# Moving the transposes of q, k and the attention output from TensorE to the DMA crossbar, from the third token block on

## The chip, the cores and the metric

The kernel runs on one core of a Trainium2 chip. The metric is the device time in microseconds (us). The engines are named as in the profile: PE is TensorE (matmuls), PEld its weight loads, DVE is VectorE, ACT is ScalarE, POOL is GpSimd and SP is SyncE, which in this kernel does nothing but issue DMA transfers, one after the other in a fixed order. "L234" is line 234 of the kernel that the profile belongs to.

Each kernel was run several times. All comparisons below are of fast runs; one run counted as slow (of `g6_early_ring_store`, 365.85 us) and is left out of its ratio.

## The reference, cut to what matters

```python
# q, k, v: (8, 8, 576, 64) float32; w_in: (512, 2048); w_out: (2048, 512)
scores = scale * q @ k.T                       # per batch and head
mask   = (rel >= 0) & (rel < 64)               # sliding window of 64, causal
attn   = softmax(where(mask, scores, -1e9))
x      = (attn @ v) laid out as (4608 tokens, 512)
out    = square(maximum(x @ w_in, 0)) @ w_out
```

## The kernel before

The 4608 tokens are 36 tiles of 128 tokens, and 4 tiles make a block of 512 tokens; there are 9 blocks, numbered 0 to 8. In phase g the kernel runs the second FFN matmul (`ops`) of block g-1 and the first (`hps`) of block g on TensorE, weaves the attention of block g+1 in between, and loads q, k and v of block g+2. The order of the instructions on each engine is fixed when the kernel is built.

The score matmuls read q and k with the head dimension over the partitions (`sc<-qT,kT 64*128` in the timelines), and the first FFN matmul reads the attention output x with its 512 columns over the partitions, in four parts (`hps<-xT,w_in_sb 128*128`), so all three are transposed. Before the change TensorE does it, with an identity as second operand, into PSUM. VectorE and ScalarE copy the results back to SBUF.

```python
def load(i):                                    # tile i: three loads on SP, then casts on GpSimd
    for (src, nm) in ((k, "k"), (q, "q"), (v, "v")):
        st = stage.tile([P, H, D], FP32, name=f"{nm}_st", tag="st")
        nc.sync.dma_start(out=st[:], in_=src[b0, :, ...].rearrange("h p d -> p h d"))
    ...                                         # (a tile on the seam of two batches takes two loads each)
    nc.gpsimd.tensor_copy(out=k16s[i][:], in_=...)          # float16 copies k16, q16, v_ev, v_od
    ...

def transposes(i):
    ps = ps_att.tile([P, 2, HP, P], FP16, name="qkT_ps", tag="ps_a")
    for s, src in enumerate((k16s, q16s)):
        for hp in range(HP):                    # HP = 4
            nc.tensor.transpose(out=ps[:, s, hp, :], in_=src[i][:, hp * P:(hp + 1) * P],
                                identity=ident[:])
    kT = attw.tile([P, HP, 192], FP16, name="kT", tag="kT")
    if i > 0:                                   # the last 64 columns of the tile before
        nc.vector.tensor_copy(out=kT[:, :, 0:64], in_=kTs[i - 1][:, :, P:192])
    ...
    nc.vector.tensor_copy(out=kT[:, :, 64:192], in_=ps[:, 0])
    qT = attw.tile([P, HP, P], FP16, name="qT", tag="qT")
    nc.scalar.activation(out=qT[:], in_=ps[:, 1], func=AF.Copy, scale=1.0)

def to_xT(i):
    xt = ps_att.tile([P, DMC, P], FP16, name="xt_ps", tag="ps_a")
    for c in range(DMC):                        # DMC = 4
        nc.tensor.transpose(out=xt[:, c, :], in_=xs[i][:, 2 * c:2 * c + 2, :], identity=ident[:])
    nc.vector.tensor_copy(out=xT_of(i // 4)[:, :, (i % 4) * P:(i % 4 + 1) * P], in_=xt[:])

def ffn_out(g):
    ...
    nc.sync.dma_start(out=out[...], in_=osb[:])  # the store is on SP too

for g in range(NTB + 1):                        # NTB = 9
    streams = []
    if g > 0:        streams.append((ffn_out(g - 1), 0.0, 1.0))
    if g < NTB:      streams.append((ffn_up(g), 0.0, 1.0))
    ...
    if g + 1 < NTB:  streams.append((attention(g + 1), 0.0, 0.95))
    if g + 2 < NTB:  streams.append((loads(g + 2), 0.6 if g == 0 else 0.0, 1.0))
    for s in weave(*streams):
        s()
```

The softmax here doesn't subtract the row's maximum and nothing guards it: scores larger than these inputs give would overflow.

## Time and profile before

| before the change | value | read from |
|---|---|---|
| time, median of 4 runs | 351.89 us (351.73 to 352.61) | the runs |
| TensorE busy | 322.0 us, 92% of the span | page, part 1 |
| one token block | 34.0 us | timeline of PE |
| time of one transposed tile (3 packs of 4) on PE | 0.67 us | timeline of PE |
| DMA engines, mean busy share | 57% | page, part 3 |
| TensorE idle between 84 and 310 us | 0.05 us | windows |

The first lines are from the page of the kernel before: busy time by engine; then the span in 40 slices of 8.8 us, each digit a busy share in tenths (PEclk is the granted TensorE clock); then the DMA queue with packets, MB and its share of the 16 engines' time; then the chain of waits that ended last, by engine.

```profile
PE 322.0 (92%) x2736; PEld 161.3 (46%) x2736; DVE 202.0 (57%) x485; ACT 180.9 (51%) x321; POOL 118.3 (34%) x196
...
PE   1458786999999999999999999999999999999995
...
PEclk9999898799999999999999999999999999999999
DMA  8927995799999456838999779400000000100021
...
q1 hardware_dynamic: 122304, 46.15, 56.9%
...
PE 82%; DMA 5%; DVE 4%; POOL 4%; ACT 2%; issue 1%; SPq 1%; ACTq 0%; POOLq 0%
```

TensorE is at 90% or more in every slice from the ninth to the last but one, at full clock, and it is 82% of the chain that ended last: it is the limit. The DMA engines fall idle after slice 26: by about 227 us all of q, k and v has been loaded, so the loads run ahead of their use.

The next lines are the timeline of PE in the kernel before (start, duration, engine, line, operation, destination from sources, shapes, count).

```profile
183.38 0.39 PE L166 MATMUL qkT_ps<-ident,k_2666 128*128 128x128 f16 x4
183.61 0.39 PE L166 MATMUL qkT_ps<-ident,q_2668 128*128 128x128 f16 x4
183.83 1.03 PE L261 MATMUL ops<-w_out_sb,h_2165 128*128 128x512 f16 x4
```

Matmuls overlap, so a pack of four transposes costs the distance from its start to the next start, 0.22 to 0.23 us, and not its 0.39 us. A tile has three packs.

### The profile page before, as it was taken

What the parts mean: (1) busy time and instruction counts of PE and PEld (TensorE: products, weight loads), DVE (VectorE), ACT (ScalarE), POOL (GpSimd) and SP (SyncE); (2) the same over time, 40 slices, a digit from 0 to 9 for tenths busy, and PEclk for the clock granted to TensorE, in tenths of its full rate; (3) what the DMA queues carried; (4) which work ended last, traced back from release to release, by engine and by line L of the source; (5) the groups of instructions that cost most, each with busy time, mean ns of one, the idle gap of its engine ahead of it and who ended that gap; (6) DMA issues with size and microseconds to landing.
All of it is one profiled execution on the core that took longest, in us unless ns stands there. A gap on an engine that the chain in (4) does not pass through costs nothing.

```text
span 351.8 us, 7118 instructions
## 1 busy us (share of the span) xinstructions
PE 322.0 (92%) x2736; PEld 161.3 (46%) x2736; DVE 202.0 (57%) x485; ACT 180.9 (51%) x321; POOL 118.3 (34%) x196
## 2 busy tenths in 40 slices
PE   1458786999999999999999999999999999999995
PEld 0343234544555445544554454445445544444442
DVE  1464358545967665667576756665576566643300
ACT  2346666695646444654555355536653664344421
POOL 5960175008867334426576634440000000000000
PEclk9999898799999999999999999999999999999999
DMA  8927995799999456838999779400000000100021
GB/s 176 219 106 227 219 216 158 217 267 208 219 243 229 91 122 156 181 95 190 199 203 184 155 156 202 108 32 32 30 32 30 33 32 30 61 31 30 32 81 69
DMA packets 122338, 46.60 MB, mean 132 GB/s; under 512 B 113600, under 2 KB 113600, under 8 KB 122304
## 3 DMA queue, kind: packets, MB, share of 16 engines
q1 hardware_dynamic: 122304, 46.15, 56.9%
q8 instruction: 21, 0.34, 0.4%
q14 instruction: 13, 0.11, 0.1%
HBM read 36.70 MB, written 9.44 MB: 131 GB/s over the span
## 4 chain that ended last, share of the span: by engine, by line
PE 82%; DMA 5%; DVE 4%; POOL 4%; ACT 2%; issue 1%; SPq 1%; ACTq 0%; POOLq 0%
PE ops L261 36%; PE hps L243 33%; PE av L204 4%; PE qkT_ps L166 4%; DMA k_st<-in_k_dram 3%; PE xt_ps L217 2%; DMA ws<-in_moe_w_in_dram 2%; ACT hrelu L247 1%; DVE h_580 L248 1%; DVE x_sb L209 1%; SPq L144 1%; DVE kT L173 1%; ACT qT L175 1%; DVE h_1086 L248 0%; DVE rden L208 0%
## 5 line engine op out<-in xcount | busy, mean ns | idle before, releaser
L243 PE MATMUL hps<-xT,w_in_sb 128*128 128x512 f16 x576 | 152.0, 385 | 5.6 <-DVE h_580 L248 4.7
L247 ACT ACTIVATE hrelu<-hps 128x512 f32<-128x512 f32 x144 | 85.8, 597 | 110.2 <-PE hps L243 109.4
L243 PEld LDWEIGHTS <-w_in_sb 128*128 128x128 f16 x576 | 56.5, 99 | 73.9 <-issue 10.3
L266 ACT ACTIVATE osb<-ops 128x512 f32<-128x512 f32 x36 | 21.5, 599 | 20.5 <-PE ops L261 20.5
L175 ACT ACTIVATE qT<-qkT_ps 128x512 f16<-128x512 f16 x36 | 21.5, 596 | 19.7 <-DVE kT L173 19.7
L173 DVE COPY kT<-qkT_ps 128x512 f16<-128x512 f16 x36 | 15.2, 422 | 26.1 <-PE qkT_ps L166 26.1
L209 DVE TENSOR_TENSOR x_sb<-av,rden 128x256 f16<-128x256 f32 x72 | 27.7, 415 | 0.3
L219 DVE COPY xT<-xt_ps 128x512 f16<-128x512 f16 x36 | 15.1, 420 | 15.3 <-PE xt_ps L217 15.3
L208 DVE RECIPROCAL rden<-av 128x4 f32<-128x4 f32 x72 | 11.9, 180 | 16.7 <-PE av L204 16.5
L248 DVE SCALAR_TENSOR_TENSOR h_4808<-hps,hrelu 128x512 f16<-128x512 f32 x16 | 11.1, 692 | 16.6 <-ACT hrelu L247 16.6
L261 PE MATMUL ops<-w_out_sb,h_580 128*128 128x512 f16 x64 | 19.4, 399 | 0.0
L248 DVE SCALAR_TENSOR_TENSOR h_580<-hps,hrelu 128x512 f16<-128x512 f32 x16 | 11.0, 690 | 13.1 <-ACT hrelu L247 13.1
L184 PEld LDWEIGHTS <-kT 64*128 64x128 f16 x576 | 11.7, 99 | 14.9 <-issue 12.4
L261 PE MATMUL ops<-w_out_sb,h_1086 128*128 128x512 f16 x64 | 16.7, 380 | 0.0
L261 PE MATMUL ops<-w_out_sb,h_2165 128*128 128x512 f16 x64 | 16.5, 380 | 0.0
L261 PE MATMUL ops<-w_out_sb,h_1627 128*128 128x512 f16 x64 | 16.5, 380 | 0.0
L261 PE MATMUL ops<-w_out_sb,h_3244 128*128 128x512 f16 x64 | 16.5, 380 | 0.0
L261 PE MATMUL ops<-w_out_sb,h_2706 128*128 128x512 f16 x64 | 16.5, 380 | 0.0
L261 PE MATMUL ops<-w_out_sb,h_3785 128*128 128x512 f16 x64 | 16.5, 380 | 0.0
L261 PE MATMUL ops<-w_out_sb,h_4322 128*128 128x512 f16 x64 | 16.4, 379 | 0.0
L248 DVE SCALAR_TENSOR_TENSOR h_1086<-hps,hrelu 128x512 f16<-128x512 f32 x16 | 11.0, 688 | 9.1 <-ACT hrelu L247 9.1
L217 PE MATMUL xt_ps<-ident,x_sb 128*128 128x128 f16 x144 | 15.8, 236 | 0.3 <-DVE x_sb L209 0.3
(743 smaller groups left out, 549.2 us busy)
## 6 DMA issues: line engine op xcount, KB each, us to landing
out_dram<-osb SPq DMA_DIRECT2D x36, 256.0 KB, 2.1
k_st<-in_k_dram SPq DMA_DIRECT2D x32, 256.0 KB, 4.6
q_st<-in_q_dram SPq DMA_DIRECT2D x32, 256.0 KB, 4.8
v_st<-in_v_dram SPq DMA_DIRECT2D x32, 256.0 KB, 4.7
ws<-in_moe_w_in_dram SPq DMA_DIRECT2D x16, 256.0 KB, 4.3
k_st<-in_k_dram SPq DMA_DIRECT2D x8, 128.0 KB, 3.9
q_st<-in_q_dram SPq DMA_DIRECT2D x8, 128.0 KB, 3.7
v_st<-in_v_dram SPq DMA_DIRECT2D x8, 128.0 KB, 3.4
```

The source lines that it names most:

```text
L166: nc.tensor.transpose(out=ps[:, s, hp, :], in_=src[i][:, hp * P:(hp + 1) * P], identity=ident[:])
L173: nc.vector.tensor_copy(out=kT[:, :, 64:192], in_=ps[:, 0])
L175: nc.scalar.activation(out=qT[:], in_=ps[:, 1], func=AF.Copy, scale=1.0)
L204: nc.tensor.matmul(av[64 * blk:64 * blk + 64, h % 4, 0:65], pms[i][h % 2][:, h // 2, blk, :], vv[:, h, 0:65], start=True, stop=True)
L209: nc.vector.tensor_tensor(out=x_sb[:, 4 * half:4 * half + 4, :], in0=av[:, :, 0:D], in1=rden[:].to_broadcast([P, 4, D]), op=ALU.mult)
L217: nc.tensor.transpose(out=xt[:, c, :], in_=xs[i][:, 2 * c:2 * c + 2, :], identity=ident[:])
L219: nc.vector.tensor_copy(out=xT_of(i // 4)[:, :, (i % 4) * P:(i % 4 + 1) * P], in_=xt[:])
L243: nc.tensor.matmul(hps[:], w_in_sb[:, c, f * P:(f + 1) * P], xT_of(g)[:, c, :], start=(c == 0), stop=(c == DMC - 1))
L247: nc.scalar.activation(out=hrelu[:], in_=hps[:], func=AF.Relu)
L248: nc.vector.scalar_tensor_tensor(out=h2s[g][:, f, :], in0=hps[:], scalar=0.0, in1=hrelu[:], op0=ALU.max, op1=ALU.mult)
L261: nc.tensor.matmul(hold["ps"][:], h2s[g][:, f, ts * P:(ts + 1) * P], w_out_sb[:, f, :], start=(f == 0), stop=(f == FFC - 1))
L266: nc.scalar.activation(out=osb[:], in_=hold["ps"][:], func=AF.Copy, scale=OUT_SCALE)
```

## The change

The intent is to take the transposes of 28 of the 36 tiles from TensorE, the limit, and to give them to the DMA engines, which have room on average (57% busy). The first two blocks keep TensorE; in their time the DMA engines also carry the weights (issued from 13.7 to 74.6 us in SP's timeline; the first slices of the DMA row above).

```diff
+    GPE = 2
@@
-    def transposes(i):
+    def transposes_pe(i):
     ...                                         # unchanged, for blocks 0 and 1
+    def transposes(i):
+        kT = attw.tile([P, HP, 192], FP16, name="kT", tag="kT")
+        if i > 0:
+            nc.vector.tensor_copy(out=kT[:, :, 0:64], in_=kTs[i - 1][:, :, P:192])
+        ...
+        nc.sync.dma_start_transpose(out=kT[:, :, 64:192], in_=k16s[i][:])
+        qT = attw.tile([P, HP, P], FP16, name="qT", tag="qT")
+        nc.sync.dma_start_transpose(out=qT[:], in_=q16s[i][:])
@@
-    def to_xT(i):
+    def to_xT_pe(i):
     ...
+    def to_xT(i):
+        nc.sync.dma_start_transpose(
+            out=xT_of(i // 4)[:, :, (i % 4) * P:(i % 4 + 1) * P],
+            in_=xs[i][:].rearrange("p h d -> p (h d)"))
@@
-        fns = (transposes, scores, values, to_xT)
+        if g < GPE:
+            fns = (transposes_pe, scores, values, to_xT_pe)
+        else:
+            fns = (transposes, scores, values, to_xT)
@@
-            streams.append((attention(g + 1), 0.0, 0.95))
+            streams.append((attention(g + 1), 0.0, 0.95 if g + 1 < GPE else 0.8))
```

So SP issues 84 more DMA instructions of 128 KB, 12 in each block, in one queue with the loads and the stores. The attention of a block is woven in a little earlier (0.8 in place of 0.95), to leave time for the last transpose.

More of the change, by code (lines that the diff above doesn't have):

```diff
@@ L175, in transposes @@
         nc.scalar.activation(out=qT[:], in_=ps[:, 1], func=AF.Copy, scale=1.0)
+        kTs[i], qTs[i] = kT, qT
+    def transposes(i):
[3 more added lines that the diff above has]
+        else:
+            nc.vector.memset(kT[:, :, 0:64], 0.0)
+        nc.sync.dma_start_transpose(out=kT[:, :, 64:192], in_=k16s[i][:])
+        qT = attw.tile([P, HP, P], FP16, name="qT", tag="qT")
+        nc.sync.dma_start_transpose(out=qT[:], in_=q16s[i][:])
         kTs[i], qTs[i] = kT, qT
@@ L219, in to_xT @@
         nc.vector.tensor_copy(out=xT_of(i // 4)[:, :, (i % 4) * P:(i % 4 + 1) * P], in_=xt[:])
+    def to_xT(i):
+        nc.sync.dma_start_transpose(
+            out=xT_of(i // 4)[:, :, (i % 4) * P:(i % 4 + 1) * P],
+            in_=xs[i][:].rearrange("p h d -> p (h d)"))
     def attention(g):
         steps = []
-        fns = (transposes, scores, values, to_xT)
+        if g < GPE:
+            fns = (transposes_pe, scores, values, to_xT_pe)
+        else:
+            fns = (transposes, scores, values, to_xT)
         for t in range(4 + len(fns) - 1):
```

## The prediction

> **What bounds the kernel now.** TensorE. In the 40-slice row PE is at 90% or more from slice 9 on (about 70 us), with a granted clock of 1.0; the chain of waits that ended last is PE for 82%. In the PE timeline around 180 to 220 us there is no gap: a token block takes 34.0 us (first k transpose of one block at 183.4 us, of the next at 217.4 us). VectorE (57%) and ScalarE (51%) have room. The DMA engines are busy for 57% of the span on average, but for 64 to 109% in the stretches from 75 to 215 us, because q, k, v arrive in 256-byte packets.
>
> **What the change removes.** 28 of the 36 tiles lose 12 PE transposes, one 422 ns VectorE copy of k, one 420 ns copy of xT and one 596 ns ScalarE copy of q. The mean busy time of a transpose (236 ns) overstates it, since they are pipelined: in the timeline a pack of four holds PE for 0.22 us (183.38 to 183.61 to 183.83 us). So a tile loses 3 x 0.225 = 0.67 us of PE, 28 tiles 18.9 us, all on the critical path: the ceiling is about 333 us. The 24 us of VectorE and 17 us of ScalarE that go free are worth nothing there.
>
> **What it adds.** 84 crossbar transposes of 128 KB on the SP queue, in order with the loads and stores. Per block of about 32 us SP then issues 12 to 15 loads (0.4 to 1.3 us each in the SP timeline, about 9 us), 4 stores (0.36 us) and 12 transposes. [...] So SP, not the DMA engines, is the likeliest new limit; it also blocks in order on output tiles (174 us of its waits before) and on x_sb.
>
> **The order.** In the instruction orders the last values step of a block is five out/up pairs (about 8.6 us) before the next block's first up matmul, against two before; that is to cover the last xT transpose. Block 2 is worse: its up matmuls come after all 64 out matmuls of block 1, and then in long runs. Runs of up matmuls wait for VectorE (1.1 us gaps near 41 and 49 us before). I expect 3 to 6 us lost there.
>
> **Sum.** 352 - 19 + 4 (block 2) + 7 (waits for late kT, qT, xT while loads run, before about 240 us) = 344 us. Range 331 to 385. Faster by over 2%: 0.47; within 2%: 0.23; slower: 0.30.
>
> **What would show it.** Right: the qkT and xt groups shrink to 8 tiles; the block period falls to about 31.8 us in the last attention blocks, which have no loads; the remaining loss shows as PE waits for DMA transposes or hps between 100 and 240 us[...]. Wrong: block period at 34 us or more also in the last attention blocks; or PE idle little and the time near 333.
>
> **What would make it wrong.** A transpose that costs SP or the engines 3 us or more: 12 of them exceed a block, the program becomes bound by that queue and takes 370 us or more. Or transposes so cheap that nothing waits: 333 us.

The sum came to 344 us (352 - 19 + 4 + 7), with 333 us as the ceiling.

## More of the kernel before

The windows view gives the busy time of each engine in stretches that are named; this is its last line for seven stretches from 84 to 310 us, in the kernel before.

```profile
sum 226.00, PE 225.95 PEld 113.64 DVE 149.75 ACT 119.41 POOL 81.91; mean PE 32.28 PEld 16.23 DVE 21.39 ACT 17.06 POOL 11.70
```

In those 226 us TensorE is idle for 0.05 us. The same line is used below for every kernel.

## The result, and the profile after

The changed kernel takes 356.63 us (median of 4 runs, 356.43 to 356.93) against 351.89 us. The ratio is 1.0131, with a 95% interval of 1.0114 to 1.0149: 1.3% slower, which is within 2%. Ratios here are the mean time of one kernel's fast runs over that of the other's of the same rounds, so they are not quite the ratio of the medians quoted.

The page of the changed kernel, the same lines as before:

```profile
PE 308.5 (87%) x2400; PEld 144.0 (41%) x2400; DVE 175.9 (50%) x429; ACT 165.9 (47%) x293; POOL 116.3 (33%) x196
...
PE   1467778999996879988999998799999989999996
...
PEclk9999996999999998999999999899999999999999
DMA  9937996989869989988899999996999832110012
...
q1 hardware_dynamic: 168000, 57.17, 78.6%
...
PE 41%; DMA 28%; SPq 10%; POOL 8%; DVE 5%; ACT 3%; issue 3%; POOLq 0%; DVEq 0%; ACTq 0%
```

TensorE did lose work: 2,400 matmul instructions in place of 2,736. But it now has slices of 6, 7 and 8, and is only 41% of the chain; DMA transfers and SP's issuing have become 38% of it. The DMA engines are busy to about 280 us. If the difference of their shares is put down to the added transposes, 78.6% of 354.5 us less 56.9% of 351.8 us is 78.5 us, or 0.93 us of all 16 engines for each of the 84. That is an estimate: the same subtraction for `e1_unread` below, which issues the same 84, gives 0.83 us.

The windows view of the changed kernel, the same stretches; of the single stretches, only 116 to 148 us and the last line are shown (columns: length, then busy time and instructions of each engine, granted clock, DMA share, GB/s).

```profile
116.00:148.00 32.00, 28.33 (x231) 12.57 (x230) 18.15 (x44) 15.21 (x27) 12.26 (x20) 0.95 0.98 191
...
sum 226.00, PE 208.01 PEld 94.76 DVE 121.68 ACT 104.11 POOL 78.51; mean PE 29.72 PEld 13.54 DVE 17.38 ACT 14.87 POOL 11.22
```

TensorE is idle for 17.99 us where it was idle for 0.05 us. Of these, 8.42 us fall between 84 and 148 us (the first crossbar block and the start of the second), and 9.57 us between 148 and 310 us. That nearly uses up the 18.9 us that were taken off it. The granted clock was 0.95 in two of the seven stretches (116 to 148 us above, and 212 to 244 us), where it was 1.00 in all seven before: an estimated 3 us more.

The largest gap, and a later one, in the timeline of PE of the changed kernel (the bracket gives the idle time before an instruction, and what ended it):

```profile
111.55 0.38 PE L281 MATMUL ops<-w_out_sb,h_1086 128*128 128x512 f16 x1
115.75 0.60 PE L263 MATMUL hps<-xT,w_in_sb 128*128 128x512 f16 x2 [3.82 <-DMA xT<-x_sb]
...
133.16 0.24 PE L196 MATMUL sc_1846<-qT,kT 64*128 64x64 f16 x3 [2.69 <-DMA qT<-q_1539]
```

And what SP issued just before, in its own timeline:

```profile
104.65 2.55 SPq L234 DMA_TRANSPOSE xT<-x_sb  x2
107.26 0.57 SPq L145 DMA_DIRECT2D k_st<-in_k_dram  x1
107.89 0.58 SPq L145 DMA_DIRECT2D q_st<-in_q_dram  x1
108.51 0.59 SPq L145 DMA_DIRECT2D v_st<-in_v_dram  x1
109.20 1.22 SPq L288 DMA_DIRECT2D out_dram<-osb  x1
110.52 2.69 SPq L234 DMA_TRANSPOSE xT<-x_sb  x2
...
129.30 1.22 SPq L187 DMA_TRANSPOSE qT<-q_1539  x1
```

From 104 to 134 us SP works without a break of more than 0.17 us. The two last transposes of x are issued from 110.52 to 113.21 us, behind three loads and a store; their data lands at 115.75 us, and TensorE has stood since 111.93 us. (The last x itself was late: VectorE could write it only at 107.91 us, after 3.18 us of waiting for a buffer that the transposes issued at 104.65 us still had to read.) A single transpose takes 1.22 us of SP (median of 65 that the timeline shows singly, smallest 1.19 us). The transpose of q_1539 at 129.30 us makes the next gap: PE waits 2.69 us for it, until 133.16 us. From 134.31 to 137.72 us, soon after this gap, the granted clock was 0.50. After the gap of 3.82 us it was 1.00 (windows, 115.7 to 119 us), and eight matmuls took 1.90 us. So in this trace the length of a gap alone does not tell whether the clock falls.

This is an estimate of SP's demand in a block, from median issue times of this trace: 12 transposes of 1.22 us, 4 loads each of k (0.58), q (0.58) and v (0.93 us), 4 stores of 0.57 us make 25.3 us. With some 0.08 us between any two of the 28 instructions it is about 27.5 us, before any seam tile and before any wait for an output tile. A block without transposes should take TensorE 34.0 - 4 x 0.67 = 31.3 us. So by this estimate SP has under 4 us of slack in a block.

The waits of VectorE and TensorE for crossbar data tell how late the data is. Before the change there are none. In the changed kernel VectorE waits 15.7 us for transposes (13 waits: copies of the 64-column tail of kT, and x tiles that wait for a buffer), and TensorE 14.5 us (10 waits).

### The profile page after: what moved, and what is told of

Read it like the earlier page. It is cut to its first block, busy times and chain, and to the rows that moved or that the text cites. A ratio compares the mean times of both kernels' runs of the same rounds, so it can differ in the third digit from the quotient of the medians.

```text
span 354.5 us, 6536 instructions
## 1 busy us (share of the span) xinstructions
PE 308.5 (87%) x2400; PEld 144.0 (41%) x2400; DVE 175.9 (50%) x429; ACT 165.9 (47%) x293; POOL 116.3 (33%) x196
## 3 DMA queue, kind: packets, MB, share of 16 engines
q1 hardware_dynamic: 168000, 57.17, 78.6%
## 4 chain that ended last, share of the span: by engine, by line
PE 41%; DMA 28%; SPq 10%; POOL 8%; DVE 5%; ACT 3%; issue 3%; POOLq 0%; DVEq 0%; ACTq 0%
PE ops L281 18%; PE hps L263 18%; DMA v_st<-in_v_dram 14%; SPq L145 4%; PE av L216 3%; SPq L234 3%; DMA q_st<-in_q_dram 3%; DMA k_st<-in_k_dram 2%; ACT hrelu L267 2%; DMA ws<-in_moe_w_in_dram 1%; DMA qT<-q_2896 1%; SPq L187 1%; DMA kT<-k_1071 1%; DMA qT<-q_3378 1%; DMA kT<-k_3861 1%
## 5 line engine op out<-in xcount | busy, mean ns | idle before, releaser
L263 PEld LDWEIGHTS <-w_in_sb 128*128 128x128 f16 x576 | 55.5, 99 | 79.0 <-issue 13.2
L221 DVE TENSOR_TENSOR x_sb<-av,rden 128x256 f16<-128x256 f32 x72 | 28.5, 418 | 4.0 <-DMA xT<-x_sb 3.6
L268 DVE SCALAR_TENSOR_TENSOR h_1086<-hps,hrelu 128x512 f16<-128x512 f32 x16 | 11.1, 692 | 17.2 <-ACT hrelu L267 17.2
L268 DVE SCALAR_TENSOR_TENSOR h_4416<-hps,hrelu 128x512 f16<-128x512 f32 x16 | 11.1, 692 | 16.6 <-ACT hrelu L267 16.6
L268 DVE SCALAR_TENSOR_TENSOR h_1571<-hps,hrelu 128x512 f16<-128x512 f32 x16 | 11.0, 686 | 15.5 <-ACT hrelu L267 15.5
L220 DVE RECIPROCAL rden<-av 128x4 f32<-128x4 f32 x72 | 11.5, 176 | 14.1 <-PE av L216 13.7
L268 DVE SCALAR_TENSOR_TENSOR h_2538<-hps,hrelu 128x512 f16<-128x512 f32 x16 | 10.9, 687 | 13.2 <-ACT hrelu L267 13.1
L268 DVE SCALAR_TENSOR_TENSOR h_3020<-hps,hrelu 128x512 f16<-128x512 f32 x16 | 11.1, 691 | 12.3 <-ACT hrelu L267 12.2
L268 DVE SCALAR_TENSOR_TENSOR h_580<-hps,hrelu 128x512 f16<-128x512 f32 x16 | 11.0, 690 | 11.3 <-ACT hrelu L267 11.3
L268 DVE SCALAR_TENSOR_TENSOR h_3505<-hps,hrelu 128x512 f16<-128x512 f32 x16 | 11.0, 688 | 8.9 <-ACT hrelu L267 8.8
L281 PE MATMUL ops<-w_out_sb,h_1086 128*128 128x512 f16 x64 | 15.4, 380 | 0.0
```

The costliest lines, as they stand in the source:

```text
L220: nc.vector.reciprocal(out=rden[:], in_=av[:, :, 64:65])
L221: nc.vector.tensor_tensor(out=x_sb[:, 4 * half:4 * half + 4, :], in0=av[:, :, 0:D], in1=rden[:].to_broadcast([P, 4, D]), op=ALU.mult)
L263: nc.tensor.matmul(hps[:], w_in_sb[:, c, f * P:(f + 1) * P], xT_of(g)[:, c, :], start=(c == 0), stop=(c == DMC - 1))
L268: nc.vector.scalar_tensor_tensor(out=h2s[g][:, f, :], in0=hps[:], scalar=0.0, in1=hrelu[:], op0=ALU.max, op1=ALU.mult)
L281: nc.tensor.matmul(hold["ps"][:], h2s[g][:, f, ts * P:(ts + 1) * P], w_out_sb[:, f, :], start=(f == 0), stop=(f == FFC - 1))
```

## The experiments

Four theories were to be told apart.

- SP ISSUE: SP's time for each transpose instruction, in one queue with the loads and stores, makes kT, qT and xT late.
- ENGINES: the 16 DMA engines have no room for the added bytes.
- IN-ORDER VECTOR: the copy of the kT tail, in order on VectorE, waits for the DMA and holds up the evacuation of `hps`.
- LATE XT: the transpose of x is too close to its use.

The expectations also name ORDER (TensorE's own order of instructions is to blame), LEAD (too little time between issue and use), and FULL QUEUE (SP or the DMA engines, not told apart).

Kernels of a group below shared chip and runs of the kernel before, whose median was 351.8 to 352.5 us in each group. A difference between kernels changes the build-time order of instructions too. How far the order of matmuls agrees is said where it matters.

### The added transfers without their use, and the loads

`e1_unread` is the kernel before plus all 84 transposes, into tiles that nobody reads.

```diff
+        if i >= 8:
+            for src in (k16s, q16s):
+                scr = scrp.tile([P, HP, P], FP16, name="scr", tag="scr")
+                nc.sync.dma_start_transpose(out=scr[:], in_=src[i][:])
   ...                                           # the same for x in to_xT
```

> The kernel before, all its TensorE transposes kept, with the same 84 crossbar transposes added on the SP queue into tiles that nobody reads. Theory SP (the queue that issues is full: 1.21 us a transpose): the SP queue is busy without a pause from about 85 us on, loads finish later than the 227 us of before, and the time rises to 355 to 365. Theory ENGINES (the 16 DMA engines are full): the same, with a DMA share near 1.0 until about 280 us. Theory WAITS (only the waits of TensorE for late qT, kT, xT cost): nobody waits here, so 351 to 353.

Measured: 353.08 us (351.82 to 354.34), ratio 1.0022 (0.9983 to 1.0061): nothing is lost, as only WAITS expected. These are lines of its page (DMA slices and queue) and the last line of its windows view.

```profile
DMA  9927996999869999988789996999699431210012
...
q1 hardware_dynamic: 168000, 57.17, 76.7%
```

```profile
sum 226.00, PE 224.32 PEld 112.42 DVE 144.96 ACT 116.90 POOL 78.99; mean PE 32.05 PEld 16.06 DVE 20.71 ACT 16.70 POOL 11.28
```

The engines and SP carry the same transfers as in the changed kernel at the old pace of 34 us a block, and TensorE is idle for 1.68 us. What costs time is not that the transfers exist. It is that something waits for them, at a pace that would be faster.

`e2_loads_pool` is the changed kernel with the loads of q, k and v issued from GpSimd (`nc.gpsimd.dma_start` in `load`), to free SP.

> The changed kernel with the loads of q, k and v issued from GpSimd, so that SP issues only transposes, stores and weights. Theory SP: SP's load falls from about 30 to 18 us a block, transposes issue as soon as their input is there, and the time falls to 335 to 343. Theory ENGINES: the same bytes in the same packets, DMA share still near 1.0 in 105 to 278 us, time 350 to 362. Theory WAITS/ORDER: between the two, 340 to 350, with PE gaps before the second block's up matmuls as in the changed kernel.

Measured: 403.82 us, ratio 1.1458. GpSimd's busy time went from 116 to 213 us; TensorE started later, and waited 28.6 us for qT. All three expectations missed. The edit costs more than it could show, so it is inconclusive.

`e3_2kb_after` and `e3_2kb_before` give a wrong result. They read q, k and v in rows of 2 KB in place of 256 bytes, at the same bytes, so that the loads cost the engines and SP less: the queue's share of the engines' time is 39.5% in `e3_2kb_before` and 56.9% in the kernel before, at 46.15 MB in both, and a load takes 0.43 us on SP in the median.

```diff
-            if j0 + 1 < NB:
+            if True:
                 nc.sync.dma_start(
-                    out=st[:], in_=src[b0, :, 64 * j0:64 * j0 + P, :].rearrange("h p d -> p h d"))
+                    out=st[:], in_=src.rearrange("b h (s t) d -> (b h s) (t d)", t=8)[i * P:(i + 1) * P, :]
+                        .rearrange("p (h d) -> p h d", h=H))
```

> Wrong result on purpose: the changed kernel reads q, k and v as rows of 2 KB instead of pieces of 256 bytes (same bytes, same number of DMAs, another layout of the data). Theories SP and ENGINES both: both resources are relieved, the transposes are no longer late, and the kernel is 15 to 20 us faster than its counterpart without crossbar transposes (e3_2kb_before). Theory ORDER (TensorE's instruction order or too short a lead is to blame, whatever the traffic): it stays within 8 us of that counterpart.

> Control, wrong result on purpose: the kernel before with q, k and v read as rows of 2 KB. All theories: TensorE bounds it from about 70 us on, so only the start gains, 342 to 351.

Measured: 342.23 us (341.31 to 343.68) for the control and 346.83 us (344.28 to 347.65) with the change, both with faster loads. So the change still costs 4.6 us there, as ORDER expected. Only about half of the order of its matmuls agrees with the changed kernel's (by its trace), so it is no clean test of the traffic either. In the windows the TensorE idle time of `e3_2kb_after` is 12.65 us, all of it before 180 us. Up to 148 us the engines are full (a share of 0.96 and 1.06 in the two stretches): the cheaper loads run further ahead there, in the same queue as the transposes. That the transposes come late behind them is only argued. From 180 us on, where the share is 0.52 and less (0.99 to 1.04 up to 276 us in the changed kernel), TensorE has no idle time. Cheaper loads alone do not bring the gain.

### Stores elsewhere, transposes earlier

`e6_store_act` is the changed kernel with the stores issued from ScalarE (`nc.scalar.dma_start`). `f4_early_store` does that, and issues the transposes of q and k in the load stream, a block ahead of their use:

```diff
+    def tq(i):
+        kTs[i] = ktp.tile([P, HP, 192], FP16, name="kTe", tag="kTe")
+        nc.sync.dma_start_transpose(out=kTs[i][:, :, 64:192], in_=k16s[i][:])
+        qTs[i] = qtp.tile([P, HP, P], FP16, name="qTe", tag="qTe")
+        nc.sync.dma_start_transpose(out=qTs[i][:], in_=q16s[i][:])
     def transposes(i):
+        nc.vector.tensor_copy(out=kTs[i][:, :, 0:64], in_=kTs[i - 1][:, :, P:192])
     ...                                          # loads(g) calls tq(i - 1) after load(i)
```

`f5_early_qk` is `f4_early_store` with x transposed on TensorE again (56 crossbar transposes).

> The changed kernel with only its 36 stores issued from ScalarE instead of SP (an edit of one line). Theory SP (the queue was busy for 95 to 100% of 84 to 273 us): a block's issues shrink by 4 stores of 0.55 to 1.2 us, about 3 us of 31, and in-order blocking on osb goes away; SP's share falls to about 0.9, the waits of TensorE for qT shrink, and the time falls to 343 to 352. Theory ENGINES: bytes unchanged, 355 to 358. Theory ORDER: the instruction order of the block-2 transition is unchanged in kind, so its loss of about 10 us stays and the time is 350 to 357.

> The kernel of e6_store_act in which the crossbar transposes of q and k are issued with the loads, one block ahead of their use (9 and 8 buffers), so that no wait for qT or kT is left on TensorE or VectorE; SP still issues all 84. Theory SP alone: as e6_store_act, 343 to 352, since the issues are the same. Theory LEAD (too little time between issue and use): waits for qT and kT vanish, 334 to 343. Theory ENGINES: 352 to 358.

> As f4_early_store, but the attention output is transposed on TensorE again: 56 crossbar transposes, 12.6 us of TensorE saved in place of 18.9. SP has 8 transposes a block (about 24 us of issues in 31 to 33). Theory LEAD or SP: both exposures are gone, 339 to 344 and a version faster than both kernels. Theory ENGINES: DMA work falls by a third of what was added, 348 to 354.

Measured: 360.53, 357.37 and 343.98 us; ratios 1.0244, 1.0136 and 0.9774 (0.9751 to 0.9797). Four issues a block off SP, and a block of distance for q and k, do not help as long as all three transposes stay on SP: VectorE then waited 31.6 and 38.4 us for crossbar data. With x on TensorE it does help, and this was the first version shown to be over 2% faster than the kernel before. That `e6_store_act` is slower, not faster, than the changed kernel doesn't fit SP ISSUE well. No expectation held for it. Its matmuls come in a different order (77% in common with the changed kernel), so the two effects are not separated. TensorE idles about as long as in the changed kernel (19.63 us between 84 and 310 us), but the granted clock is below 1.00 in four of the seven stretches (0.89 at the least), an estimated 5 us more lost: that is about what it is slower by.

### Fewer crossbar blocks

`e4_gpe6` sets `GPE = 6`, `e4_gpe4` sets `GPE = 4`: the change in the last 12 and the last 20 tiles alone. The second was run in a later group.

> The change switched on only from the seventh block on (12 tiles instead of 28): the blocks whose attention runs with few loads left. Theories SP and ENGINES: nothing is full there, so each of three blocks gains most of its 2.7 us: 344 to 347. Theory LEAD/ORDER: a wait for kT, qT or xT in each of the three blocks takes it back: 348 to 353.

> The changed kernel from the fifth block on alone (20 tiles, ideal gain 13.4 us: 338.5). Its order of matmuls in those blocks is the regular four and four. If the loss lies in the first crossbar blocks and their order: 338 to 341 us. If it lies in the blocks that run beside loads, whichever they are: blocks 4 to 6 lose 1 to 3 us each and it takes 342 to 347 us, no better than e4_gpe6.

Measured: 344.19 us for `GPE = 6`, ratio 0.9780 (0.9752 to 0.9808), 7.6 us better than the kernel before, where 12 x 0.67 = 8.1 us could be had. For `GPE = 4` it is 352.47 us, ratio 1.0004: of 13.4 us nothing is left, which neither expectation held. The regular order of its matmuls did not save it. This is the line of VectorE's waits in `e4_gpe4` (total us, times, longest):

```profile
DVE kT L182 <- DMA kT<-k: 25.4, 13, 5.4
```

In `e4_gpe6` the same line shows 1.3 us. Blocks 4 and 5, which `e4_gpe4` adds, issue their transposes while the loads are in full flow. With `GPE = 6` the loads could run ahead before the first transpose (SP's timeline is filled to 0.41 and 0.52 in the stretches from 116 to 180 us, where in `e4_gpe4` it is filled to 0.55 and 0.90).

### The copy of the k tail

`h3_store_ring` is `e6_store_act` with k of a whole block in one tile of 576 columns, so that 7 tail copies on VectorE remain of 28. The order of its matmuls is that of `e6_store_act` exactly.

```diff
     def transposes(i):
+        j = i % 4
+        if j == 0:
+            kTs[i] = (ktp.tile([P, HP, 576], FP16, name="kTb", tag="kTb"), 0)
+            pt, po = kTs[i - 1]
+            nc.vector.tensor_copy(out=kTs[i][0][:, :, 0:64], in_=pt[:, :, po + P:po + 192])
         else:
+            kTs[i] = (kTs[i - 1][0], P * j)
+        kt, o = kTs[i]
+        nc.sync.dma_start_transpose(out=kt[:, :, o + 64:o + 192], in_=k16s[i][:])
     ...                                          # scores reads k at the offset o; store on ScalarE
```

`g2_2kb_ring` is the same ring in `e3_2kb_after` (wrong), `g6_early_ring_store` in `f4_early_store`. `h2_mixed` is `g6_early_ring_store` with x on the crossbar from block 6 on only.

> The kernel of e6_store_act with one edit: the transposed k of a block lies in one tile of 576 columns, so only the first tile of a block needs the VectorE copy of the 64 columns before it (7 copies in place of 28). TensorE's instruction order is the same instruction for instruction. Theory IN-ORDER VECTOR (VectorE stands in those copies, 30.3 us in e6_store_act, until the crossbar transpose of k lands, and cannot empty TensorE's result banks meanwhile): the waits of TensorE for VectorE (11.5 us of hps, 2.7 at most) mostly vanish and the time falls by 5 to 10 us, to 350 to 356. Theory FULL QUEUE (SP and the DMA engines at 95 to 100% set the pace): the wait moves to the scores' wait for kT and qT, and the time stays within 2 us of 360.5.

> Wrong result on purpose, as e3_2kb_after, with the same single edit as h3_store_ring; TensorE's order is the same as in e3_2kb_after. Here neither SP nor the DMA engines are full. Theory IN-ORDER VECTOR: the 16.6 us that VectorE stood in the copies shrink to under 5, the three TensorE gaps of 1.2 to 2.4 us behind VectorE vanish, and the time falls from 346.8 to 334 to 341, below its control of 342.2. Theory LEAD OF xT (the last transposes of a block come too late for the next block): 344 to 347.

> The kernel of f4_early_store (q and k transposed one block ahead, stores from ScalarE, all 84 crossbar transposes) with the same edit. Theory IN-ORDER VECTOR: 35.8 us of VectorE's standing fall below 10; 340 to 350. Theory FULL QUEUE: 354 to 358.

> A version meant to beat both kernels: q and k from block 2 on through the crossbar, one block ahead, into the tile of 576 columns; the attention output through the crossbar only from block 6 on, when the loads are nearly over; stores from ScalarE. Removed from TensorE: 28 x 0.45 + 12 x 0.225 = 15.3 us. If no new wait appears (all theories, since neither SP nor the DMA engines are needed beyond f5_early_qk): 337 to 342. If the last blocks wait for xT: 342 to 346.

Measured: 364.73, 351.30, 358.25 and 348.26 us. The three kernels with the edit alone are no faster than theirs without it (360.53, 346.83 and 357.37 us), and `h2_mixed` is slower than either expectation. The premise of `g2_2kb_ring`, that neither SP nor the DMA engines are full, was not shown for the whole span: in `e3_2kb_after` the engines' share was 0.96 and 1.06 up to 148 us. With a quarter of the copies, VectorE still waited, 20.9 us in 5 waits (from `h3_store_ring`) where `e6_store_act` had 30.3 us in 16:

```profile
DVE kTb L185 <- DMA kTb<-k: 20.9, 5, 6.1
```

So taking copies away does not help. That they only show that the data is late is argued here, since VectorE still stood for 20.9 us; `j1_merge` below, which keeps all 28 copies and gains, supports it. `h2_mixed` lost part of the gain of `f5_early_qk`, with gaps of 1.7 and 3.1 us near 202 and 231 us.

### Which transpose, and what SP pays for

`e5_qk_only` puts the transpose of x back on TensorE, `e5_xt_only` those of q and k:

```diff
-            fns = (transposes, scores, values, to_xT)
+            fns = (transposes, scores, values, to_xT_pe)        # e5_qk_only
+            fns = (transposes_pe, scores, values, to_xT)        # e5_xt_only
```

> The changed kernel with the transpose of x put back on TensorE: 56 crossbar transposes in place of 84, none early, stores still on SP. The ideal gain is 28 x 0.45 = 12.6 us: 339.5. If the late xT is what loses the gain (theory LATE XT): 343 to 346 us, as f5_early_qk. If the demand on SP and the DMA engines loses it (theory FULL QUEUE), two thirds of the demand leaves SP about 25 us a block, and it is also below 346. If q and k, late at the scores, lose it: 350 us or more, with PE waits for qT or for the VectorE copy of the k tail of over 8 us.

> The changed kernel with the q and k transposes put back on TensorE: 28 crossbar transposes, of x alone. The ideal gain is 28 x 0.22 = 6.2 us: 345.7. SP issues only 4 transposes a block and the DMA engines have room, so FULL QUEUE expects 346 to 348 us. LATE XT expects the waits for xT to stay (4 us or more) and 349 to 354 us.

Measured: 356.09 us (353.91 to 356.79) and 346.99 us (345.82 to 347.58). With x alone, 5.5 of the 6.2 us possible are gained, and TensorE idles for 0.43 us between 84 and 310 us. LATE XT falls as the main cause. With q and k alone nothing is gained; VectorE waited 10.6 us for kT. So there q and k, two thirds of the instructions, are what comes late. Against SP ISSUE it can be said that 8 transposes a block should have been bearable (by the estimate above, 27.5 us less 4 x 1.3 us, about 22 us of SP a block). Its matmul order is also another (74% in common with the changed kernel).

`j1_merge` changes only how many instructions move q and k. The float16 copies of k and q of a tile lie side by side, and one instruction transposes both, 256 KB at once. That makes 56 instructions in place of 84, at the same bytes.

```diff
-        k16s[i] = st16.tile([P, H * D], FP16, name="k16", tag="k16")
+        kq = st16.tile([P, 2, H * D], FP16, name="kq16", tag="kq16")
+        kqs[i] = kq
+        k16s[i], q16s[i] = kq[:, 0, :], kq[:, 1, :]
@@ def transposes(i):
-        kT = attw.tile([P, HP, 192], FP16, name="kT", tag="kT")
-        ...
-        nc.sync.dma_start_transpose(out=kT[:, :, 64:192], in_=k16s[i][:])
-        qT = attw.tile([P, HP, P], FP16, name="qT", tag="qT")
-        nc.sync.dma_start_transpose(out=qT[:], in_=q16s[i][:])
+        kqT = attw.tile([P, 2 * HP, 192], FP16, name="kqT", tag="kqT")
+        nc.vector.tensor_copy(out=kqT[:, 0:HP, 0:64], in_=kTs[i - 1][:, 0:HP, P:192])
+        nc.sync.dma_start_transpose(out=kqT[:, :, 64:192],
+                                    in_=kqs[i][:].rearrange("p s d -> p (s d)"))
+        kTs[i], qTs[i] = kqT, kqT[:, HP:2 * HP, 64:192]
```

> The changed kernel with k and q of one tile transposed by one instruction of 256 KB: 56 instructions in place of 84, the same bytes. If SP pays by instruction, the merged one takes about 1.2 us of SP, SP has 5 us a block more room, and FULL QUEUE expects 350 us or less. If SP pays by bytes, it takes about 2.4 us, and the time stays within 2% of the changed kernel's. The landing should be later than that of a single one, 4 us or more.

Measured: 341.10 us (339.68 to 342.42), ratio 0.9679 (0.9640 to 0.9719). That is 15 us better than the changed kernel (from runs of another group), and the lowest time. The sequence of its matmuls by kind differs from the changed kernel's in 2 of 2,400 places, so this comparison is clean, and ORDER cannot be what the 15 us come from. From its page, its windows and its timelines of PE and SP:

```profile
DMA  9937898679999999999899599999989714100021
...
q1 hardware_dynamic: 167104, 57.17, 81.1%
```

```profile
sum 226.00, PE 221.98 PEld 101.86 DVE 130.62 ACT 110.56 POOL 81.48; mean PE 31.71 PEld 14.55 DVE 18.66 ACT 15.79 POOL 11.64
```

```profile
113.16 1.90 PE L261 MATMUL hps<-xT,w_in_sb 128*128 128x512 f16 x8 [0.71 <-DMA xT<-x_sb]
```

```profile
179.46 1.24 SPq L184 DMA_TRANSPOSE kqT<-kq  x1
180.75 0.57 SPq L146 DMA_DIRECT2D k_st<-in_k_dram  x1
181.37 0.62 SPq L146 DMA_DIRECT2D q_st<-in_q_dram  x1
```

And from its list of DMA transfers (the last number is the median time from issue to landing, in us):

```profile
kqT<-kq SPq DMA_TRANSPOSE x28, 4.2
```

The DMA engines are as full as in the changed kernel (57.17 MB, 81.1%), which rules ENGINES out as the cause. SP issues 256 KB in 1.24 us (that is the shortest of the 28; their median, waits included, is 1.35 us), about what it needed for 128 KB. The gap ahead of the first up matmul of block 2 is 0.71 us in place of 3.82 us, TensorE's idle time 4.02 us in place of 17.99 us, and the waits for crossbar data are 1.2 us on VectorE (before: 15.7 us) and 0.7 us on TensorE (before: 14.5 us). The last load has landed at about 262 us in place of 277 us.

`j3_merge_dummy` gives the issue time back. After each merged transpose SP issues one of a single 128 x 128 piece, 32 KB, into a tile that nobody reads. `j4_merge_x` goes the other way and transposes the x of two tiles with one instruction.

```diff
# j3_merge_dummy = j1_merge and
+        scr = scrp.tile([P, 1, P], FP16, name="scr", tag="scr")
+        nc.sync.dma_start_transpose(out=scr[:], in_=kqs[i][:, 1, 0:P])
# j4_merge_x = j1_merge and (xT laid out as [P, 4, DMC, P])
+        if i % 2 == 1:
+            t = i % 4
+            nc.sync.dma_start_transpose(
+                out=xT_of(i // 4)[:, t - 1:t + 1].rearrange("p t c k -> p (t c) k"),
+                in_=xps[i // 2][:].rearrange("p t h d -> p (t h d)"))
```

> j1_merge plus, after each merged transpose, one transpose of a single 128x128 piece (32 KB) into a tile that nobody reads: again 12 transpose instructions a block on SP, 8% more bytes. If SP's time for an instruction is what cost the changed kernel its gain (theory SP ISSUE), the small one also takes about 1.2 us of SP and the time goes back to 350 us or more. If what helped was that k and q land together as one larger transfer (theory ONE TRANSFER), it stays at 340 to 344 us. The order of matmuls differs a little from j1_merge's (95% in common), which may be worth 1 to 2 us.

> j1_merge with the x of two tiles transposed by one instruction too (the layout of xT becomes tile by tile): 6 transpose instructions a block in place of 8, the same bytes. SP ISSUE expects 337 to 341 us, at most a little better than j1_merge, since little PE idle time is left there; if the pair's later landing matters more, PE waits for xT appear and it takes 342 us or more.

Measured: `j3_merge_dummy` 364.47 us (362.53 to 366.67), ratio 1.0360 (1.0324 to 1.0397). So 28 instructions, which add 8% to the bytes of the transposes and which nobody waits for, cost 23 us. From its timeline of SP, its list of transfers, its windows, and its timeline of PE:

```profile
185.73 1.23 SPq L188 DMA_TRANSPOSE scr<-kq  x1
187.06 1.25 SPq L185 DMA_TRANSPOSE kqT<-kq  x1
188.36 1.23 SPq L188 DMA_TRANSPOSE scr<-kq  x1
```

```profile
q1 hardware_dynamic: 171584, 58.09, 74.0%
...
kqT<-kq SPq DMA_TRANSPOSE x28, 3.9
```

```profile
sum 226.00, PE 206.99 PEld 93.42 DVE 120.47 ACT 101.40 POOL 79.67; mean PE 29.57 PEld 13.35 DVE 17.21 ACT 14.49 POOL 11.38
```

```profile
116.68 5.30 PE L264 MATMUL hps<-xT,w_in_sb 128*128 128x512 f16 x12 [3.81 <-DMA xT<-x_sb]
```

The transpose of 32 KB holds SP for 1.23 us, as long as one of 256 KB. The idle time of TensorE is back at 19.01 us, the gap ahead of block 2 at 3.81 us (the twelve matmuls after it took 5.30 us, so 0.44 us each, against 0.24 us for the eight after the 3.82 us of the changed kernel), and VectorE and TensorE wait 15.4 and 12.1 us for crossbar data, nearly as in the changed kernel. The DMA engines are less busy than in `j1_merge` (74.0%), and the merged transpose lands no later after its issue (3.9 us, against 4.2 us): in the median, the added instructions do not slow the transfers down. What `j1_merge` gained is thus the issue time, not the merged transfer. This kernel is 8 us slower than the changed one. Of these, an estimated 5 us are the clock: it was 0.80 from 116 to 148 us, where the changed kernel had 0.95, and 0.95 from 276 us on. The rest may lie in the order of matmuls, of which 95% agrees, or in k and q landing together; this was not separated.

`j4_merge_x` took 342.60 us (341.25 to 342.90), ratio 0.9739: no better than `j1_merge`, and above the 337 to 341 us that SP ISSUE expected. TensorE waits only 0.4 us for xT, so a later landing of the pair doesn't explain it. Its idle time, 5.50 us, is no less either. At the 8 transposes a block of `j1_merge` little is left to gain on SP.

## Why the prediction was right or wrong, point by point

- That TensorE bounds the kernel before: right. Where the crossbar data came in time, the work taken off showed in the time nearly in full: 7.6 of 8.1 us (`e4_gpe6`), 5.5 of 6.2 us (`e5_xt_only`).
- "So a tile loses 3 x 0.225 = 0.67 us of PE, 28 tiles 18.9 us, all on the critical path": right in size, and right as a ceiling. Of the 18.9 us `j1_merge` keeps 11.4 us (352.53 less 341.10), the changed kernel as given none.
- What a transpose costs SP: the estimate held. Measured, it is 1.22 us, so 12 make 14.6 us of SP a block, about 27.5 us with the rest by the estimate above.
- What the added transposes cost the engines: this estimate was too small. From the shares measured it is an estimated 0.83 to 0.93 us each, 69 to 78.5 us in all. That the engines bear it is shown by `e1_unread` (ratio 1.0022) and `j1_merge` (0.9679), with the same bytes.
- "SP, not the DMA engines, is the likeliest new limit": right. `j1_merge` and `j3_merge_dummy` show it (28 instructions fewer: 15 us faster; 28 of 32 KB back: 23 us slower).
- "The block period falls to about 31.8 us in the last attention blocks, which have no loads": not tested as meant. The loads no longer run ahead and last to 277 us, so no attention block but the last is without loads. The prediction had overlooked that a full SP queue delays the loads too.
- **The step that failed** is the sum: "+ 4 (block 2) + 7 (waits for late kT, qT, xT while loads run ...)". What would wait, and for what, was right; the size was not. The waits cost about 22 us in place of 11, and both terms were about half of what came: block 2 cost an estimated 8.5 us in place of 4, the rest 13.4 us in place of 7. The working follows.
  - Block 2: the mark is the start of VectorE's last evacuation of that block's first FFN half. The changed kernel is there 7.4 us late (144.7 against 137.3 us). The mix of work at the mark differs too. By the traces TensorE has been spared the transposes of q and k of 9 tiles and of x of 8 (5.9 us), but has run 24 `ops` matmuls more (156 in place of 132) and 2 `hps` fewer, an estimated 4.8 us at 0.216 us each. So it had 1.1 us less to do, and lost 7.4 + 1.1 = 8.5 us.
  - The rest: from there to the same mark of block 8 it took 193.2 us against 197.6 us. That is 4.4 us gained of the other 18.9 - 1.1 = 17.8 us, so 13.4 us were lost.
  - With 22 us in place of 11 the sum 352 - 19 + 22 gives 355 us, about what was measured. In `j1_merge`, which has done the same work at both marks, the two terms are 2.0 and 4.3 us: some 15.6 us of the 21.9 us lost go away when SP's issues do.

The prediction had SP's list for a block (12 to 15 loads, 4 stores, 12 transposes) next to a block of about 32 us in its own text, named SP the likeliest new limit, and still entered 7 us for it. A queue that is nearly full (by the estimate above 27.5 of 31.3 us), in front of in-order consumers, was treated as a small correction. The change as given is within 2% of the kernel before; with one transpose instruction for k and q it is 3.2% faster.

Four things stay open. `e5_qk_only` (8 transposes a block) and `e6_store_act` (four stores fewer on SP) gained nothing, though both take issue time off SP; their instruction orders differ from the changed kernel's, and no run separated the two effects. SP's share of time is no measure by itself: in `e1_unread` and `j1_merge` it is as high as in the changed kernel (0.9 and more in most stretches), because issues that have to wait are counted with it (two merged transposes near 263 us of `j1_merge` are shown with 6.16 us; in all, its merged transposes waited 17.7 us, 11 times, for a cast of k on GpSimd). And the 6 us between `j1_merge` (339.2 us profiled) and the ceiling (351.8 - 18.9 = 332.9 us) are only in part its 4.02 us of idle time; by the marks above 2.0 us of them are lost by block 2. And no run gave the x of the changed kernel more buffers, though VectorE waited up to 3.2 us for one there.

## What to carry to other kernels

Count DMA instructions, not only bytes: here SP paid 1.2 us for a crossbar transpose whether it moved 32, 128 or 256 KB (1.23, 1.22 and 1.24 us where nothing held it up), so merge transposes until the issuing queue has clear slack in the shortest block that you hope for. Work that is moved off the bounding engine is gained only where its result arrives in time (here 11.4 of 18.9 us with `j1_merge`, nothing with the change as given): ask what stands ahead of it in its queue, above all loads that used to run ahead. To test such a queue, change the number of instructions at constant bytes, and keep the order on the bounding engine the same; experiments that changed the order here gave answers that could not be separated.
